# One kernel for sliding-window attention and an S4 convolution: all exponentials of a chunk ahead of its sines

## The chip, the cores and the metric

The kernel runs on one core of a Trainium2 chip. The metric is the time on the device in microseconds of one execution of the whole program; the median of several executions is given. The work is done by five engines that run side by side and wait for each other by semaphores: PE (matrix multiply, with its weight loads shown as PEld), DVE (vector), ACT (activation functions and copies), POOL, and SP, which only issues transfers. Each engine works through its own instructions in a fixed order.

## The reference

Two independent parts share the launch and their results stand side by side in the output.

Part A is attention with 32 heads of 20 over 2048 positions, where each position looks at eight earlier ones, two apart. It is a projection to q, k, v, eight logits per position, a softmax and an output projection.

Part B is a long convolution with a filter that is computed on the fly:

```python
dt = jnp.exp(log_dt)[:, None]
logdA = dt * A                                   # A complex, 640 x 192
dB = dt * Bc
P = jnp.exp(logdA[:, :, None] * l[None, None, :])  # l = 0..2047
K = jnp.einsum("dn,dnl,dn->dl", Cc, P, dB).real    # the filter, 640 x 2048
...                                               # FFT of length 4096 of K and u, product, inverse
y = y + u * Dskip
```

The exponential of a complex number is an exponential of the real part (a magnitude) times a cosine and a sine of the imaginary part (an angle). The kernel therefore needs both Exp and Sin from ACT.

## The kernel before

**Chunks and halves.** The 640 channels of part B are cut into five chunks (`NCH`) of 128. For every chunk the 2048 filter points are made as products of two small tables: Y (32 fine offsets, twice) and X (32 coarse offsets). The coefficients of a chunk are in two halves (`th` 0 and 1, 16 of the channel rows `t` each). Each half has a Y and an X of its own place (`Y0`, `X0`, `Y1`, `X1`).

**Coefficient steps.** `prep_coef` and `prep_chunk` (L67 to L140) turn the parameters into exact pieces in 16-bit floats: `base` and `logmag` for magnitudes and angles, `phi` for the starting angle, which needs Arctan. The pieces go to memory (`scr`) and come back by `load_pieces` (L155) in two tiles: `PM` for magnitudes and `PF` for angles. Chunk 0 is handled by itself at the start; the coefficients of chunks 1 to 4 lie together in the tiles `natr` (place X1) and `cfr` (place Y1).

**Table steps.** `table_steps` (L185) makes the tables of one half in 18 steps. PE multiplies the pieces by constants (`RM`, `RF`) into a PSUM bank `ps_t`, and ACT takes the function. The first step gives the factors `E` (L216), three steps give the magnitudes `M` (L224), two give `MX` (L238), all with Exp. DVE completes M and MX with multiplies by E (L229, L240). Then come 12 sine steps (L252): for each of three blocks, cosine and sine of Y and cosine and sine of X. After each pair DVE multiplies in the magnitudes (L258 to L260 for Y by M, L264 for X by MX). `M`, `MX` and `E` have one place each, which both halves use in turn.

**Other steps.** `kgen_steps` (8 steps of matmuls, L290 and L294) multiplies X by Y for one half and copies the result to `Ksb` (L297). `fwd_steps` (8 steps) is a discrete Fourier transform in two stages: stage one (`f1`, L381) is copied to the tile `A1` (L342), stage two (`f2`, L392) to `Ssp` (L342). It runs for the input `u` (`u_steps`; the result is stored to memory in `Udram`) and for the filter `Ksb`, where DVE then multiplies it with `U`, read back from memory (L420). `ia` (4 steps, L429) is the first stage of the inverse; it is copied to `Z` and stored in `Zdram`. The second stage of the inverse (`ib`, L586) runs near the end, when `zq` is read back from `Zdram` in six groups; its weights are the constant `H`. The copies at L342 go to ACT or DVE by a letter pattern.

**The order of the work.** `interleave(a, b)` writes two lists of steps alternately. In the main loop each half's 18 table steps are interleaved with what became ready earlier: kgen of half 0, the previous chunk's `ia` and one `u_steps` during the tables of half 1; kgen of half 1 and the filter's forward steps during the tables of half 0 of the next chunk. The first list, during the sines of chunk 0, holds `u_steps(0)`, `u_steps(1)` and the coefficient steps of chunks 1 to 4. A scheduler then orders the instructions of each engine by its own model, keeping the written order as priority; `order`, `vorder` and `sorder` (L28) are chains that fix the order of chosen instructions on ACT, DVE and SP. Tiles with the same `tag` share a place, with as many copies as `bufs` says; a new tile there waits until all uses of the old one are over.

**After part B's chunks**, part A runs: projections (L657, L697), logits (L713, L716), softmax, the weighted sum (L772, L776) with `ib` between, and the output projection (L790). It uses places that part B has left: `xa` takes X0, `xb` and every second `zq` a place of their own, `S8`; `wq` takes MX, `prod` takes X1 and M, `attn` takes Z, `H` takes A1.

## Time and profile before

| | us |
|---|---|
| median of 3 runs | 535.12 (532.24 to 537.8) |
| the profiled execution | 537.6 |
| its span | 535.8 |
| DVE busy in the span | 389.2 (73%) |
| PE busy | 391.0 (73%) |
| ACT busy | 345.4 (64%) |
| first table load at L216 to the end of the last sine | 75.4 to 340.8 |

The profile is of one execution. Times count from the start of the span, which is a little shorter than the execution. A "line" is a line of the kernel; a helper such as the copy at L342 collects many tiles under one line, so groups are told apart by their tile names. An idle time is the time just before an instruction in which its engine did nothing, and the profile names the instruction that ended it. PE's ends are modelled. ACT loads a table of functions (ACT_TABLE_LOAD) whenever the next function isn't in the one it has.

### The profile page before, as it was taken

The numbers are of one execution on the slowest core, as the hardware profiler recorded it, in microseconds if no ns is written. First come the engines' busy times: TensorE is split into PE (matmuls) and PEld (weight loads), VectorE is DVE, ScalarE is ACT, GpSimd is POOL, SyncE is SP. The second block draws the span as 40 slices with busy tenths as digits, with TensorE's granted clock in tenths as the row PEclk, the third lists the DMA queues.
The fourth block names the chain that finished last, engine by engine and source line by source line (L and its number), as shares of the span: only waits on it lengthen the run. The fifth ranks groups of instructions, "written<-read, shape, count | busy, mean of one in ns | idle before, by whom it ended". The sixth has DMA issues, their size and how long they took to land.

```text
span 535.8 us, 15507 instructions
## 1 busy us (share of the span) xinstructions
PE 391.0 (73%) x7009; PEld 245.8 (46%) x7009; DVE 389.2 (73%) x420; ACT 345.4 (64%) x451; POOL 35.9 (7%) x51
## 2 busy tenths in 40 slices
PE   0214675856798858976897678799799797788687
PEld 0103553533475436643564356445444465455355
DVE  3656997938878596989885977704585999985840
ACT  2393795957889868986998669557345362633254
POOL 8700001010002001010000000000000000000000
PEclk9999877878899887988799789989999799877879
DMA  5499343280028100750016008902102004653413
GB/s 122 107 156 220 115 139 84 94 195 3 1 67 260 31 0 18 234 166 1 3 44 196 1 2 295 241 22 80 80 1 62 1 4 113 188 123 103 102 67 107
DMA packets 51706, 51.57 MB, mean 96 GB/s; under 512 B 37416, under 2 KB 48360, under 8 KB 48696
## 3 DMA queue, kind: packets, MB, share of 16 engines
q1 hardware_dynamic: 49752, 49.69, 34.3%
q0 software_dynamic: 1184, 0.89, 0.8%
q8 instruction: 55, 0.90, 0.7%
q10 hardware_dynamic: 704, 0.00, 0.1%
q14 instruction: 11, 0.09, 0.1%
HBM read 32.30 MB, written 18.19 MB: 94 GB/s over the span
## 4 chain that ended last, share of the span: by engine, by line
DVE 36%; PE 34%; ACT 15%; issue 10%; DMA 4%; ACTq 0%; SPq 0%; POOL 0%; DVEq 0%; POOLq 0%
PE ps_qk L657 6%; DVE A L342 4%; DVE Y L258 4%; PE ps_t L203 4%; PE ps_k L290 4%; DVE X L264 3%; DVE prod L772 3%; PE ps_k L294 3%; DVE Y L260 3%; ACT Y L252 3%; PE ps_op L790 3%; PE ps_ia L429 2%; ACT X L252 2%; DVE Ssp L342 2%; DVE prod L713 2%
## 5 line engine op out<-in xcount | busy, mean ns | idle before, releaser
L252 ACT ACTIVATE X<-ps_t 128x1024 bf16<-128x1024 int16 x60 | 61.5, 1055 | 4.8 <-PE ps_t L203 3.3
L252 ACT ACTIVATE Y<-ps_t 128x1024 bf16<-128x1024 int16 x60 | 61.0, 1045 | 5.5 <-PE ps_t L203 3.5
L772 DVE TENSOR_TENSOR prod<-v,attn 128x2048 bf16<-128x2048 bf16 (+1 forms) x48 | 47.4, 1041 | 15.3 <-PE ps_o L776 15.3
L203 PE MATMUL ps_t<-R,PF 128*128 128x512 f16 (+1 forms) x160 | 52.0, 415 | 1.7 <-ACT Ksb L297 0.6
L713 DVE TENSOR_TENSOR prod<-qT,kT 128x5120 bf16<-128x5120 bf16 x16 | 44.6, 2817 | 9.1 <-ACT qT L342 4.7
L203 PE MATMUL ps_t<-R,PM 128*128 128x256 f16 (+3 forms) x160 | 22.9, 272 | 36.5 <-DMA PM<-scr 23.5
L258 DVE TENSOR_TENSOR Y<-Y,M 128x2048 bf16<-128x2048 bf16 x30 | 36.6, 1220 | 15.4 <-ACT Y L252 15.4
L342 DVE CAST A<-ps_f 128x1024 bf16<-128x1024 f32 x28 | 34.1, 1219 | 15.8 <-PE ps_f L381 15.8
L342 ACT CAST Ssp<-ps_f 128x1024 bf16<-128x1024 f32 x26 | 26.5, 1019 | 19.4 <-PE ps_f L392 19.4
L294 PE MATMUL ps_k<-Y,X 64*32 64x64 bf16 x1280 | 26.5, 235 | 16.5 <-issue 16.5
L264 DVE TENSOR_TENSOR X<-X,MX 128x2048 bf16<-128x2048 bf16 x30 | 36.6, 1219 | 0.2
L260 DVE TENSOR_TENSOR Y<-Y,M 128x2048 bf16<-128x2048 bf16 x30 | 36.6, 1218 | 0.2
L776 PE MATMUL ps_o<-prod,ident 32*32 32x512 bf16 (+1 forms) x768 | 24.1, 388 | 14.8 <-DVE prod L772 12.3
L381 PE MATMUL ps_f<-BD,u 128*64 128x128 bf16 x320 | 21.8, 290 | 17.5 <-DMA BD<-c_BD 12.0
L203 PEld LDWEIGHTS <-PM 128*128 128x128 f16 (+1 forms) x160 | 13.9, 102 | 44.4 <-DMA PM<-scr 23.5
L294 PEld LDWEIGHTS <-X 64*32 64x32 bf16 x1280 | 19.9, 116 | 30.1 <-issue 29.5
L381 PEld LDWEIGHTS <-u 128*64 128x64 bf16 x320 | 19.7, 204 | 25.5 <-issue 25.5
L224 ACT ACTIVATE M<-ps_t 128x1024 bf16<-128x1024 f32 x30 | 28.5, 1026 | 3.9 <-DVE Y L260 3.9
L420 DVE TENSOR_TENSOR U<-U,Ssp 128x2048 bf16<-128x2048 bf16 x20 | 24.3, 1221 | 9.0 <-ACT Ssp L342 9.0
L392 PE MATMUL ps_f<-A,WK 128*128 128x128 bf16 x160 | 16.5, 265 | 18.2 <-DVE A L342 18.2
L290 PE MATMUL ps_k<-Y,X 128*32 128x64 bf16 x1280 | 24.4, 242 | 5.7 <-ACT Ssp L342 1.9
L206 PE MATMUL ps_t<-R,PF 128*64 128x512 f16 (+1 forms) x160 | 27.4, 433 | 1.7 <-ACT Ssp L342 0.9
(146 smaller groups left out, 795.0 us busy)
## 6 DMA issues: line engine op xcount, KB each, us to landing
Udram<-Ssp SPq DMA_DIRECT2D x5, 1024.0 KB
U<-Udram SPq DMA_DIRECT2D x5, 1024.0 KB
U<-Udram SPq DMA_DIRECT2D x10, 512.0 KB
Zdram<-Z SPq DMA_DIRECT2D x5, 1024.0 KB
zq<-Zdram SPq DMA_DIRECT2D x25, 192.0 KB
u<-in_B_u_dram SPq DMA_DIRECT2D x4, 640.0 KB
xn<-in_A_x_dram SPq DMA_DIRECT2D x4, 640.0 KB
out_dram<-ob SPq DMA_DIRECT2D x16, 160.0 KB
```

Of the source, the lines that this page charges most:

```text
L203: MM(ps, lhsT=Pt[0:K, 2 * blk + th, 0:128], rhs=rhs[0:K], start=True, stop=True, skip_group_check=True)
L252: order(nc.scalar.activation(out=dst, in_=ps[:].bitcast(i16)[:, :, 0::2].rearrange("p i (k z) -> p (i k) z", z=128), func=ACT.Sin, scale=S ...
L258: V.tensor_tensor(out=hi, in0=lo, in1=m(0), op=A.mult)
L260: V.tensor_tensor(out=lo, in0=lo, in1=m(1), op=A.mult)
L264: V.tensor_tensor(out=xf, in0=xf, in1=mx, op=A.mult)
L290: MM(o, lhsT=X[:, r, 4 * g + t // 4, :, t % 4], rhs=Y[:, r, 4 * g + t // 4, :, t % 4], start=(k == 0 and r == 0), stop=False, tile_positio ...
L294: MM(o, lhsT=X[hb:hb + 64, r, kq, :, t % 4], rhs=Y[hb:hb + 64, r, kq, :, t % 4], start=False, stop=(r == 1), tile_position=(hb, 32 * g), s ...
L342: ins = self.nc.scalar.copy(out=out, in_=in_) if e == "a" else self.nc.vector.tensor_copy(out=out, in_=in_)
L381: MM(ps[64 * r:64 * r + 64, i], lhsT=src_fn(8 * q + i), rhs=BD[:, r], start=(i % 4 == 0), stop=True, skip_group_check=True, tile_position= ...
L657: self.nc.tensor.matmul(ps, lhsT=self.w[w][:, kt, 128 * ct:128 * ct + 128], rhs=rhs(kt), start=(kt == 0), stop=(kt == 4))
L713: self.nc.vector.tensor_tensor(out=pr[:], in0=self.qT[:, hf], in1=self.kT[:, hf, :, :, HALO - DIL * w:HALO - DIL * w + 256], op=A.mult)
L772: nc.vector.tensor_tensor(out=p2[:, 0:nd], in0=self.v2[b][:, :, off:off + 256], in1=self.attn[:, hf, w, :].unsqueeze(1).to_broadcast([128, ...
```

## The change

`table_steps` becomes a class `Tables`, made once per chunk. Its `exps()` are the 11 exponential steps of both halves (one E for both, then M and MX of half 0 and of half 1) and its `sins(th)` the 12 sine steps of one half. M and MX get a place per half (`M0`, `M1`, `MX0`, `MX1`). In the main loop the exponentials and the sines of half 0 are interleaved with kgen of half 1, the forward steps and `ia` of the previous chunk; the sines of half 1 with kgen of half 0 and one `u_steps`, which comes one chunk later than before. PM has one copy instead of two, Z takes the place of A1, the scratch tiles are joined in U's place, `S8` goes (M0 takes its users), and H is no longer held whole: each `zq` group gets its slice of H by a transfer ahead of its five others.

At the start, the coefficient products `zed0` come before `base0` and their parameters are loaded first; SP's early transfers are chained. The exponentials of both halves of chunk 0 are issued before its Arctan, a Sin on a 128x1 tile stands before that, BD is loaded before u, and the phi pieces after u. `u_steps(0)`, `u_steps(1)` and the coefficient steps of chunks 3 and 4 move to the sines of half 1 of chunk 0. The x load is a step of its list and no longer issued ahead of it.

```diff
-    PM = pools["arena"].tile([128, 8, CW], f16, name="PM", tag="PM", bufs=2)
+    PM = pools["arena"].tile([128, 8, CW], f16, name="PM", tag="PM")
...
@@ -182,23 +182,24 @@
-def table_steps(tc, pools, R, P, th, order, Y, X, rows=(128, 128), vorder=None):
-    M = pool.tile([128, 6400], bf16, name="M", tag="M", bufs=1)
-    MX = pool.tile([128, 24, 32, 4], bf16, name="MX", tag="MX", bufs=1)
-    E = pool.tile([128, 2, 24, 4], bf16, name="E", tag="E", bufs=1)
...
+class Tables:
...
+    def __init__(self, tc, pools, R, P, order, rows=(128, 128), vorder=None):
...
+        self.PF, self.PM = P
+        ar = pools["arena"]
+        self.M = [ar.tile([128, 6400], bf16, name="M", tag="M%d" % th) for th in range(2)]
+        self.MX = [ar.tile([128, 24, 32, 4], bf16, name="MX", tag="MX%d" % th) for th in range(2)]
+        self.E = ar.tile([128, 2, 2, 24, 4], bf16, name="E", tag="E")
...
-    def new():
-        return psp.tile([128, 2, 512], f32, name="ps_t", tag="b", bufs=4)
-
...
-        order(nc.scalar.activation(out=E[:].rearrange("p k (b q) t -> p b k (q t)", b=6), in_=ps[:, 0, 0:192].rearrange("p (b k t) -> p b k t", k=2, t=16), func=ACT.Exp))
-
+    def gens(self):
+        ps = self.new()
+        for th in range(2):
+            for k in range(2):
+                for blk in range(6):
+                    o = 192 * th + 96 * k + 16 * blk
+                    self.block(ps[:, 0, o:o + 16], blk, th, self.PM, self.RM[:, 768 + 16 * k:784 + 16 * k], self.rows[0])
+        self.order(self.nc.scalar.activation(out=self.E[:].rearrange("p h k q t -> p (h k q t)"), in_=ps[:, 0, 0:384], func=ACT.Exp))
...
+    def mag(self, th, b):
+        M, V = self.M[th], self.V
+
+        def run():
+            ps = self.new()
...
+            self.order(self.nc.scalar.activation(out=M[:].rearrange("p (q y) -> p q y", q=2)[:, :, 1024 * b:1024 * b + 1024].rearrange("p q (k z) -> p q k z", z=128)[:, :, :, 0:64], in_=ps[:].rearrange("p q (k z) -> p q k z", z=64), func=ACT.Exp))
...
-    steps.append(gens)
-    steps += [mag(b) for b in range(3)]
-    steps += [magx(0, 4), magx(4, 2)]
-    for b in range(3):
-        steps += [sin(b, w, cs) for w in range(2) for cs in range(2)]
-    return steps
+
+    def exps(self):
+        out = [self.gens]
+        for th in range(2):
+            out += [self.mag(th, b) for b in range(3)] + [self.magx(th, 0, 4), self.magx(th, 4, 2)]
+        return out
+
+    def sins(self, th, Y, X):
+        return [self.sin(th, Y, X, b, w, cs) for b in range(3) for w in range(2) for cs in range(2)]
...
-                st["Z"] = pool.tile([128, 128, 32], bf16, name="Z", tag="Z")[:]
+                st["Z"] = pool.tile([128, 128, 32], bf16, name="Z", tag="A1")[:]
...
-        for a in (5, 4, 0, 2, 1, 3):
-            nc.sync.dma_start(out=n0[:, a, 0], in_=psrc(a, 0))
+        for a in (0, 2, 1, 3, 5, 4):
+            sorder(nc.sync.dma_start(out=n0[:, a, 0], in_=psrc(a, 0)))
...
         for nm, x, dst in (("RM", 1, RM), ("RF", 0, RF)):
+            sorder(nc.sync.dma_start(out=dst, in_=nc.inline_tensor(table_consts_np()[x].astype(np.float16), name="c_" + nm).ap()))
...
-                (nc.sync if a in (1, 3) else nc.gpsimd).dma_start(out=nr[:, a, c - 1], in_=psrc(a, c))
+                if a in (1, 3):
+                    sorder(nc.sync.dma_start(out=nr[:, a, c - 1], in_=psrc(a, c)))
+                else:
+                    nc.gpsimd.dma_start(out=nr[:, a, c - 1], in_=psrc(a, c))
...
-        S1 = ar.tile([128, 9, CW], f32, name="scr1", tag="U")
-        S2 = ar.tile([128, 20, CW], f16, name="scr2", tag="Z")
+        S = ar.tile([128, 19 * CW], f32, name="scr", tag="U")
+        S1, S2 = S[:, 0:9 * CW].rearrange("p (k n) -> p k n", n=CW), S[:, 9 * CW:19 * CW].bitcast(f16).rearrange("p (k n) -> p k n", n=CW)
...
+        zed0()
         base0()
         load_pieces(tc, P, scr, 0, (0,), sorder)
-        zed0()
         ln0()
         logmag0()
         load_pieces(tc, P, scr, 0, (1,), sorder)
...
-        fills = table_steps(tc, pools, (RF, RM), P, 0, order, Yb[0], Xb[0], rows=(32, 64), vorder=vorder)
+        tb = Tables(tc, pools, (RF, RM), P, order, rows=(32, 64), vorder=vorder)
+        fills = tb.exps()
         for st in fills[:6]:
             st()
         expr()
+        for st in fills[6:]:
+            st()
+        BD = const_tile(tc, ar, cn["BD"], "BD", nc.sync, order=sorder)
+        u = ar.tile([128, 64, 160], bf16, name="u", tag="u")
+        for g in range(4):
+            sorder(nc.sync.dma_start(out=u[32 * g:32 * g + 32], in_=usrc[g]))
+        order(nc.scalar.activation(out=tiny[:], in_=tiny[:], func=ACT.Sin))
         angle0()
+        phi0()
+        load_pieces(tc, P, scr, 0, (2,), sorder)
         angler()
         for c in range(1, NCH):
             for a in (4, 5):
                 nc.gpsimd.dma_start(out=nr[:, a, c - 1], in_=psrc(a, c))
-        u = ar.tile([128, 64, 160], bf16, name="u", tag="u")
-        for g in range(4):
-            sorder(nc.sync.dma_start(out=u[32 * g:32 * g + 32], in_=usrc[g]))
-        BD = const_tile(tc, ar, cn["BD"], "BD", nc.sync, order=sorder)
-        phi0()
-        load_pieces(tc, P, scr, 0, (2,), sorder)
...
-        work = u_steps(0, Evac(nc, "da", dict(a=order, d=vorder)))
+        preps = []
         for c in range(1, NCH):
-            work += prep_chunk(tc, S1, S2, nr[:, 4, c - 1], nr[:, 5, c - 1], dts, lamr[:, c - 1], angr[:, c - 1], c, scr, vorder, None)
-            if c == 1:
-                work += u_steps(1)
-        interleave(fills[6:], work)
+            preps += prep_chunk(tc, S1, S2, nr[:, 4, c - 1], nr[:, 5, c - 1], dts, lamr[:, c - 1], angr[:, c - 1], c, scr, vorder, None)
+        interleave(tb.sins(0, Yb[0], Xb[0]), preps[:6])
         Yb.append(Y1())
         Xb.append(X1())
         evz = Evac(nc, "da")
+        work = u_steps(0) + u_steps(1)
+        work = [x for i in range(16) for x in ([work[i]] + (preps[6 + i // 2:7 + i // 2] if i % 2 == 0 and i < 12 else []))]
         for c in range(NCH):
             Ksb = ar.tile([128, 32, 64], bf16, name="Ksb", tag="Ksb", bufs=2)
+            done = lambda Z, c=c: nc.sync.dma_start(out=Zd[c], in_=Z.rearrange("p m t -> p (m t)"))
+            load, prod, ia = inv_steps(tc, pools, IA, Ud[c], Banks(psk, tags), evz, done)
             if c:
-                P = nextP
-            tg = tags
-            done = lambda Z, c=c: nc.sync.dma_start(out=Zd[c], in_=Z.rearrange("p m t -> p (m t)"))
-            load, prod, ia = inv_steps(tc, pools, IA, Ud[c], Banks(psk, tg), evz, done)
-            for th in range(2):
-                if c or th:
-                    interleave(table_steps(tc, pools, (RF, RM), P, th, order, Yb[th], Xb[th]), work)
-                work = kgen_steps(tc, pools, th, Yb[th], Xb[th], Ksb)
-                if th == 0:
-                    work += prev_ia if c else []
-                    if c + 2 < NCH:
-                        work += u_steps(c + 2)
-                    elif c + 2 == NCH:
-                        work.append(lambda: nc.vector.tensor_tensor(out=u[:], in0=u[:], in1=Dsb[:].unsqueeze(1).to_broadcast([128, 64, 160]), op=A.mult))
-                    else:
-                        att.load_x()
-                        work += att.transposes(lambda: psk.tile([128, 2, 512], f32, name="ps_xt", tag="b", bufs=4))
-                    if c < last:
-                        nextP = new_pieces(tc, pools)
-                        load_pieces(tc, nextP, scr, c + 1, (0, 1, 2))
-                else:
-                    load()
-                    e2 = Evac(nc, "aad") if c < last else Evac(nc, "a")
-                    work += fwd_steps(tc, pools, BD, WK, (lambda t, Ksb=Ksb: Ksb[:, t, :]), Banks(psk, tg), Evac(nc, "d" if c < last else "da"), e2, each=prod)
+                tb = Tables(tc, pools, (RF, RM), nextP, order)
+                interleave(tb.exps() + tb.sins(0, Yb[0], Xb[0]), work + prev_ia)
+                work = []
+            work = kgen_steps(tc, pools, 0, Yb[0], Xb[0], Ksb) + work
+            if 0 < c and c + 1 < NCH - 1:
+                work += u_steps(c + 1)
+            elif c == NCH - 2:
+                work += u_steps(c + 1)
+                work.append(lambda: nc.vector.tensor_tensor(out=u[:], in0=u[:], in1=Dsb[:].unsqueeze(1).to_broadcast([128, 64, 160]), op=A.mult))
+            elif c == last:
+                work.append(att.load_x)
+                work += att.transposes(lambda: psk.tile([128, 2, 512], f32, name="ps_xt", tag="b", bufs=4))
+            if c < last:
+                nextP = new_pieces(tc, pools)
+                load_pieces(tc, nextP, scr, c + 1, (0, 1, 2))
+            interleave(tb.sins(1, Yb[1], Xb[1]), work)
+            load()
+            e2 = Evac(nc, "aad") if c < last else Evac(nc, "a")
+            work = kgen_steps(tc, pools, 1, Yb[1], Xb[1], Ksb)
+            work += fwd_steps(tc, pools, BD, WK, (lambda t, Ksb=Ksb: Ksb[:, t, :]), Banks(psk, tags), Evac(nc, "d" if c < last else "da"), e2, each=prod)
             prev_ia = ia
...
-    H = const_tile(tc, ar, cn["H"], "H", nc.sync, tag="A1")
+    Hd = nc.inline_tensor(cn["H"], name="c_H").ap()
...
-                zt[0] = z = ar.tile([128, NCH, 2 * NP, 32], bf16, name="zq", tag=("X0", "S8")[l // NP % 2])
+                zt[0] = z = ar.tile([128, NCH + 1, 2 * NP, 32], bf16, name="zq", tag=("X0", "M0")[l // NP % 2])
+                nc.sync.dma_start(out=z[:, NCH, 0:2 * np_], in_=Hd[:, 2 * l:2 * (l + np_)])
                 for c in range(NCH):
                     nc.sync.dma_start(out=z[:, c, 0:2 * np_], in_=Zd[c, :, 64 * l:64 * (l + np_)].rearrange("p (m t) -> p m t", t=32))
...
-                        MM(ps[sl, 160 * i:160 * i + 160], lhsT=H[sl, m, :], rhs=z[sl, :, m - 2 * NP * (l // NP), :], start=False, stop=(r == 1),
+                        MM(ps[sl, 160 * i:160 * i + 160], lhsT=z[sl, NCH, m - 2 * NP * (l // NP), :], rhs=z[sl, 0:NCH, m - 2 * NP * (l // NP), :], start=False, stop=(r == 1),
...
-        self.xb = ar.tile([128, 2, S], bf16, name="xb", tag="S8")
+        self.xb = ar.tile([128, 2, S], bf16, name="xb", tag="M0")
...
-        for i, nm, tag in ((1, "k", "WU"), (0, "q", "MX"), (2, "v", "R")):
+        for i, nm, tag in ((1, "k", "WU"), (0, "q", "MX0"), (2, "v", "R")):
...
-            pr = self.ar.tile([128, 5, 4, 256], bf16, name="prod", tag=("X1", "M")[w % 2])
+            pr = self.ar.tile([128, 5, 4, 256], bf16, name="prod", tag=("X1", "M1")[w % 2])
...
-                self.attn = self.ar.tile([128, 2, W, 256], bf16, name="attn", tag="Z")
+                self.attn = self.ar.tile([128, 2, W, 256], bf16, name="attn", tag="A1")
...
-            p2 = self.ar.tile([128, 8, 256], bf16, name="prod2", tag=("X1", "M", "Y1")[w % 3])
+            p2 = self.ar.tile([128, 8, 256], bf16, name="prod2", tag=("X1", "M1", "Y1")[w % 3])
```

## The prediction

> **What bounds the kernel now.** I read the engine totals first, then the stretches between table loads, then what each engine waits for.
>
> ```profile
> PE 391.0 (73%) x7009; PEld 245.8 (46%) x7009; DVE 389.2 (73%) x420; ACT 345.4 (64%) x451; POOL 35.9 (7%) x51
> ```
>
> No engine is full. In the middle of the run the work repeats once per chunk, from one load of the Exp table to the next but one. The busy-time-by-stretch view of one chunk (columns: stretch, its length, busy time of PE, PEld, DVE, ACT and POOL with instruction counts, granted clock, DMA share, GB/s) gives the two halves:
>
> ```profile
> 141.86:170.89 29.03, 24.67 (x484) 18.33 (x483) 24.41 (x25) 25.60 (x28) 3.35 (x3) 1.00 0.39 117
> 170.89:200.25 29.36, 20.78 (x414) 12.01 (x414) 21.59 (x22) 22.39 (x24) 0.93 (x1) 0.88 0.15 48
> ```
>
> Together 58.4 us, with PE busy for 45.5, DVE for 46.0 and ACT for 48.0: a chunk loses about 12 us to waiting on each of the three. Cutting each half at the first multiply of its Y shows where DVE loses them:
>
> ```profile
> 170.89:182.63 11.74, 9.23 (x279) 5.63 (x279) 4.67 (x6) 9.34 (x11) 0.93 (x1) 0.85 0.37 118
> 182.63:204.95 22.32, 14.27 (x157) 8.06 (x156) 21.63 (x21) 16.80 (x19) 0.00 (x0) 0.86 0.01 1
> 200.25:213.46 13.21, 10.96 (x313) 8.20 (x312) 8.55 (x9) 10.83 (x12) 1.38 (x1) 0.74 0.08 19
> 213.46:231.29 17.83, 16.12 (x245) 11.56 (x247) 17.72 (x19) 16.38 (x18) 2.91 (x2) 1.00 0.63 202
> ```
>
> From the Exp table load to that multiply DVE idles 7.1 us in one half and 4.7 in the other, 11.7 of its 12.4. From then on it is full (21.6 of 22.3, 17.7 of 17.8). So **DVE bounds the sine part, and starves during the exponential part**, because its multiplies need a sine, and ACT does a table load, E, the M and MX exponentials and another table load first. This happens twice per chunk.
>
> **The change part by part.**
>
> *Table loads.* The groups view has 19 in the main loop:
>
> ```profile
> L252 ACT ACT_TABLE_LOAD x10 | 12.8, 1283 | 0.7 <-DVE scr L130 0.6
> ...
> L216 ACT ACT_TABLE_LOAD x9 | 11.5, 1283 | 0.2
> ```
>
> With L59, L63, L91, L97 and L748 there are 24. After it, chunk 0 needs one Exp and one sine table, chunks 1 to 4 two each; with L59, L63 and L748 that is 13, or 15 if Arctan can't use the sine table (this trace loads one for each, with Arctan first, so it can't tell; I take 13, as the Sin on `tiny` now precedes Arctan, and keep 2.6 us for the other end). ACT sheds 11 x 1.283 = 14.1 us, at worst 9 x 1.283 = 11.5. The order-of-time view shows what one load takes:
>
> ```profile
> 169.82 1.05 ACT L342 CAST Ssp<-ps_f 128x1024 bf16<-128x1024 f32 x1
> 170.89 1.28 ACT L216 ACT_TABLE_LOAD   x1
> 172.18 0.33 ACT L216 ACTIVATE E<-ps_t 128x192 bf16<-128x192 f32 x1
> ```
>
> The previous cast ends at 170.87 and the activation starts 0.01 us after the load: 1.28 us, nothing else. The Trainium skill, "ScalarE: Activation LUTs", section "What ACT_TABLE_LOAD costs", puts a switch at about 2.66 us with a drain; by it the sum would be 29 us, but no drain stands here, so the row decides.
>
> ACT is not the bound, so these 14 us are not the gain; the starved stretches are. **One longer exponential stretch per chunk replaces two.** The first stretch above (11.7 us) grows by the second half's M and MX: 2.85 + 1.54 = 4.4, so 16.1 us. DVE has 4.7 us of work in it, gains the second half's three E multiplies (2 x 0.95 + 0.95 = 2.8), and two of the four casts to A (1.14 each, back to back; 2.3), since the filter half is evacuated at 183.5, 12.6 us after the load, before the longer stretch ends. Idle: 16.1 - 4.7 - 2.8 - 2.3 = 6.3 us, for 11.7: 5.4 gained. PE doesn't forbid it: 9.2 busy plus the second half's exponential matmuls, about 3.0 (30.4 us of L203 and L206 on PM over ten halves, the narrow ones left out), makes 12.2 of 16.1. ACT no longer waits for the Y multiply before M (0.4 to 0.9 us a half), as M has a place per half.
>
> *The light second stretch.* With the half-0 sines, the inverse steps (ia) and the previous chunk's forward steps in the first, the second has the half-1 sines, kgen of half 0 and u_steps: DVE 11.6 + 4.6 = 16.2 us, but PE about 7.9 (sines) + 5.1 (kgen) + 4.4 + 2.8 (u, L381 and L392) = 20.2, plus the 2.3 us hole that PE shows inside kgen ("issue"). PE needs 22.5, DVE has 16.2 and some 4 carried over from the heavy stretch: 2 us idle. Net 3.4 us per chunk, for chunks 1 to 4: 13.6. The bounds: 0 (the idle only moves) and 7 (DVE waits for nothing in the second stretch and M's waits go too).
>
> *Start and chunk 0.* The half-1 exponentials (4.4 us of ACT) now fill the time before the phi pieces come. The price is that Arctan moves from 38.4 to about 43.5 us, and phi with it; the first X sine stays near 53, since it ran at 53.6 behind forward casts that waited for BD (12.0 us on PE). BD now goes ahead of the 16 us load of u, and u_steps(0) and (1) move behind the half-0 sines, their two 1 MB stores (at 57.9 and 71.2 on the SP queue) with them, to near 75 and 90; chunk 0's U is read back right after and wanted only some 15 us into the next stretch, so I cost that at nothing (about 5 us if it came late). A new wait: Y1 and X1 lie where cfr and natr lie, and the coefficient steps of chunks 3 and 4, which read those, now stand among the steps of the half-1 sines. They are 2 x 5.2 us of DVE (L115 to L138), and until they end every half-1 sine on ACT is held; behind them wait kgen's second half and chunk 1's exponentials. DVE has 64.8 us of work from 30.4 to 108.2 and 13.0 idle; 4.6 of the work (u_steps(2)) leaves for later. I take 4 us gained, between 6 lost (the held sines aren't covered) and 9 (two thirds of the idle gone). zed0 ahead of base0 fills DVE's 6.7 us wait for dt, but zedr still waits for natr until 19.3: nothing.
>
> *PM with one place, Z in A1's.* PM's next load can start when the exponentials end, some 40 us before its use, and its four transfers took 1.7 us to issue: free. Z is worse: the next cast to A1 waits until the store of Z has landed. The SP queue in order of time:
>
> ```profile
> 216.22 0.34 SPq L413 DMA_DIRECT2D U<-Udram  x1
> 218.74 0.34 SPq L534 DMA_DIRECT2D Zdram<-Z  x1
> 219.12 2.18 SPq L415 DMA_DIRECT2D U<-Udram  x2
> ```
>
> The U loads share the engines; DMA is full from 217 to 227, and Z (1 of 3 MB) should land by 225, 6.3 us after its issue. Between Z and the u-step casts now stands kgen of half 0, 9.3 us from the Exp load to its matmuls' end in this trace: covered, 0, at worst 6.3 a chunk. "Trainium Kernel Development and Optimization", "Best Practices", advises double buffers to overlap DMA with compute and so speaks against both; by it the 6.3 would be paid three times, 19 us. No run here shows it yet.
>
> *End.* H comes in six slices beside zq instead of one early 1 MB load, each ahead of its five zq pieces: 192 KB at the 300 to 440 GB/s of full stretches is 0.6 us plus 0.4 of issue. PE waited 0.8 us for zq at 454.6; 1 us more there. The x load is now a step behind kgen, and ia no longer covers it (322 to 327.6 before): 1 us. Together -2, between 0 and -5. PE's extra narrow matmuls in gens: under 1 us a chunk, where PE idles.
>
> **Sum.** 13.6 + 4 - 2 = 15.6 us. The profiled execution took 537.6 us (span 535.8), inside the runs' 532.2 to 537.8 but 2.5 above their median; the gain carries over, so 535.1 - 15.6 = 519.5, say **520 us**.
>
> **The rivals.**
> 1. *The idle only moves.* All three engines have 46 to 48 us of work a chunk in a fixed ring of dependencies; if kgen, forward and inverse steps set the pace, fewer table loads buy nothing: 535.1 less the 4 of chunk 0, plus the 2 of the end, 533 us. For it: PE is full from 210 to 222. Against it: DVE's idle sits in the exponentials.
> 2. *Slower: the ring through A1.* The K forward, Z, its store and the u forward now use one place in turn. From the trace: first A cast to last K matmul 183.8 to 197.7, 13.9; to the last U product 6.1; ia and its last cast 5.6; store 6.3, or kgen 9.3 if PE does it in that order; u forward 11.4 (216.6 to 228); Ksb of the next chunk, 12.6, with the second half's exponentials ahead, 4.4. All in turn: 63.3 us against 58.4, so 4.9 x 3 chunks with u_steps, chunk 0's gain gone, 2 at the end: 535.1 + 17 = 552 us. It decides once exponentials and kgen stop overlapping the u steps; without that overlap's loss the ring is 46.3 us, under the 55 I expect, which speaks against it.
> 3. *DVE full.* The upper bounds, 7 x 4 + 4 with 1 lost at the end: 504 us. PE's 45.5 busy of the 51 left speaks against it.
>
> **Numbers.** My forecast, 512 to 529: 0.45. Rival 1: 0.15. Rival 2, and lesser forms of it from 541 on: 0.22. Rival 3: 0.18. Faster by over 1% (which is about what this kernel's runs can tell from no change) is 0.45 + 0.18. The range leaves out the far ends of rivals 2 and 3: 500 to 550.
>
> **What would show it.** Right: 13 table loads; per chunk one DVE hole of about 6 us, a period near 55; no wait of an A cast for the store of Z; chunk 1's Exp load near 100 us. Wrong: A casts or f1 matmuls released by the Z store; ACT idle among the half-1 sines of chunk 0 for over 10 us; PE waits for kgen's inputs at the head of the second stretch; PE waiting over 2 us for zq.

## The result: slower, 557 us

| | median, us | ratio to before, 95% interval |
|---|---|---|
| before | 534.1 | |
| changed | 557.3 (554.8 to 566.5) | 1.041 (1.033 to 1.049) |
| predicted | 520 (500 to 550) | |

The stored profile of the changed kernel is of an execution that was disturbed (566.5 us; so is that of c below, 562.0), so its lines below come from a second profile of the same kernel, made beside the experiments (execution 563.6 us, span 561.8; median there 560.9), and the ratios leave such executions out.

The engine totals of the changed kernel, first section of its page:

```profile
PE 403.0 (72%) x7089; PEld 251.6 (45%) x7089; DVE 391.5 (70%) x420; ACT 331.8 (59%) x436; POOL 35.5 (6%) x51
```

ACT has 13.6 us less to do than before (331.8 for 345.4) and DVE about as much (391.5 for 389.2), yet the span is 26 us longer: on both the time is waiting, not work. PE is busy for 12.0 us more (403.0 for 391.0), and not by its 80 extra matmuls: j below has the same 7089 and 389.9. The groups view of table loads:

```profile
L220 ACT ACT_TABLE_LOAD x4 | 5.1, 1283 | 0.1
L260 ACT ACT_TABLE_LOAD x4 | 5.1, 1283 | 0.1
```

Together with one each at L59, L63, L91, L519 and L765 these are 13 loads for 24. The start of a chunk on ACT in order of time (start, duration, engine, line, operation, tiles) looks as it did before, one load and then E for both halves at once:

```profile
104.05 1.92 ACT L353 CAST Ssp<-ps_f 128x1024 bf16<-128x1024 f32 x2
105.99 1.28 ACT L220 ACT_TABLE_LOAD   x1
107.29 0.49 ACT L220 ACTIVATE E<-ps_t 128x384 bf16<-128x384 f32 x1
```

Where the 26 us arise is read from when the same instruction comes in the kernels: the Exp table load that starts each of the chunks 1 to 4, and the last copy to `Ksb`, after which only the last forward and inverse steps and part A remain. All are microseconds from the start of each profile's span; the labels of the other rows are explained with the experiments.

| | c1 | c2 | c3 | c4 | last Ksb | span |
|---|---|---|---|---|---|---|
| before | 108.2 | 170.9 | 229.5 | 281.6 | 351.7 | 535.8 |
| changed | 106.0 | 174.0 | 235.4 | 297.7 | 376.8 | 561.8 |
| b: ia second | 105.4 | 173.4 | 235.8 | 299.3 | 369.8 | 557.6 |
| c: Z in its own place | 104.8 | 174.1 | 236.8 | 299.0 | 378.1 | 560.3 |
| i: both, H whole | 104.7 | 164.9 | 222.4 | 277.7 | 349.1 | 535.6 |
| f: both, u_steps(0) first | 103.4 | 159.8 | 217.0 | 272.0 | 343.6 | 531.2 |
| g: both, early stores chained | 100.8 | 159.2 | 216.3 | 273.6 | 345.2 | 528.0 |
| j: both, start repaired twice | 102.2 | 160.5 | 215.4 | 271.4 | 344.6 | 527.8 |
| l: j, exponentials per half | 101.5 | 162.2 | 218.8 | 277.7 | 343.1 | 523.7 |
| n: j, per half in the last chunk | 102.0 | 160.9 | 215.8 | 271.9 | 339.1 | 522.8 |

The changed kernel is 2.2 us ahead at chunk 1 and 25.0 behind at the last Ksb. What follows adds 1. So the loss is in the chunks, all four of them (5.3, 2.8, 10.2 and 9.0 us; chunk 3 now holds a u step that chunk 2 held before).

One chunk in three stretches of the busy-time view (stretch, length, busy time of PE, PEld, DVE, ACT and POOL with instruction counts, granted clock, DMA share, GB/s): from the Exp load to a Y multiply, to the start of `ia`, and to the next Exp load:

```profile
174.02:190.86 16.84, 13.53 (x370) 9.23 (x368) 11.96 (x13) 14.79 (x17) 2.09 (x2) 1.00 0.29 91
190.86:203.44 12.58, 5.94 (x42) 3.66 (x43) 12.34 (x14) 8.34 (x9) 0.00 (x0) 0.86 0.00 0
203.44:235.38 31.94, 27.73 (x501) 18.49 (x502) 22.58 (x22) 22.03 (x24) 1.86 (x2) 0.89 0.37 102
```

The third stretch holds the last sine block of half 0 and then the "light second stretch" of the prediction: DVE has 22.6 us of work in 31.9, so it idles 9.4, where 2 were forecast for the light stretch, and PE, with 27.7 busy, isn't full either. DVE is full in the stretch before (12.3 of 12.6). PE's order of time shows what divides the chunk (in brackets the idle time before it and what ended it):

```profile
198.71 0.59 PE L204 MATMUL ps_t<-R,PF 128*128 128x512 f16 x2
203.44 1.41 PE L440 MATMUL ps_ia<-IA,U 128*128 128x128 bf16 x16 [4.14 <-DVE U L431]
204.78 1.06 PE L207 MATMUL ps_t<-R,PF 128*64 128x512 f16 x4
205.78 1.94 PE L440 MATMUL ps_ia<-IA,U 128*128 128x128 bf16 x16
207.64 0.64 PE L207 MATMUL ps_t<-R,PF 128*64 128x512 f16 x4
...
214.72 2.13 PE L301 MATMUL ps_k<-Y,X 128*32 128x64 bf16 x124
...
221.73 0.29 PE L305 MATMUL ps_k<-Y,X 64*32 64x64 bf16 x6 [2.74 <-issue]
...
224.47 2.01 PE L392 MATMUL ps_f<-BD,u 128*64 128x128 bf16 x32
```

PE stood 4.1 us in front of `ia` until the last of the four U products on DVE had ended, and the narrow sine matmuls at L207 of the half's last block stand behind `ia` in PE's queue. In the kernel before, the last product of the same chunk ended at 203.8 and `ia` began 7.3 us later, behind kgen of half 0 and table matmuls, without a wait. From its order of time, one line of DVE and then two of PE:

```profile
202.60 1.22 DVE L420 TENSOR_TENSOR U<-U,Ssp 128x2048 bf16<-128x2048 bf16 x1
...
205.39 2.11 PE L290 MATMUL ps_k<-Y,X 128*32 128x64 bf16 x124
...
211.10 1.19 PE L429 MATMUL ps_ia<-IA,U 128*128 128x128 bf16 x16
```

The wait costs more than its length. The busy-time view of the changed kernel, for the wait, the 4.6 us behind it and the next 4 (the granted clock is the third number from the end):

```profile
199.30:203.44 4.14, 0.00 (x1) 0.00 (x1) 4.14 (x6) 2.11 (x3) 0.00 (x0) 1.00 0.00 0
203.44:208.00 4.56, 4.56 (x40) 3.19 (x40) 3.35 (x3) 1.27 (x2) 0.00 (x0) 0.63 0.02 5
208.00:212.00 4.00, 4.00 (x46) 2.57 (x42) 2.51 (x3) 3.54 (x4) 0.00 (x0) 1.00 0.00 0
```

PE comes out of the wait at 0.63 of its clock, and the first four matmuls at L207 take 1.06 us where the next four take 0.64. So ACT runs dry, as its own order of time shows (4.5 us before the first sine of that block):

```profile
200.30 1.10 ACT L260 ACTIVATE X<-ps_t 128x1024 bf16<-128x1024 int16 x1
205.89 1.02 ACT L260 ACTIVATE Y<-ps_t 128x1024 bf16<-128x1024 int16 x1 [4.48 <-PE ps_t L207]
```

Later in the same stretch kgen of half 0 has PE nearly to itself, with a hole that ends with "issue", and DVE's order of time shows 5.0 us without work, until a sine comes:

```profile
217.85 1.22 DVE L272 TENSOR_TENSOR X<-X,MX 128x2048 bf16<-128x2048 bf16 x1
224.08 1.23 DVE L266 TENSOR_TENSOR Y<-Y,M 128x2048 bf16<-128x2048 bf16 x1 [5.02 <-ACT Y L260]
225.63 1.23 DVE L353 CAST A<-ps_f 128x1024 bf16<-128x1024 f32 x1 [0.33 <-PE ps_f L392]
```

The SP queue in order of time shows what happened to the transfer that the prediction feared:

```profile
211.17 0.34 SPq L424 DMA_DIRECT2D U<-Udram  x1
212.21 0.34 SPq L549 DMA_DIRECT2D Zdram<-Z  x1
212.60 1.36 SPq L426 DMA_DIRECT2D U<-Udram  x2
```

Z's store is issued at 212.2 and the next cast to A1 on DVE comes at 225.6, released by a matmul and not by the store: 13.4 us, so in this kernel the store is covered.

### The profile page after: what moved, and what is told of

Read it like the earlier page. It is cut to its first block, busy times and chain, and to the rows that moved or that the text cites. A ratio compares the mean times of both kernels' runs of the same rounds, so it can differ in the third digit from the quotient of the medians.

```text
span 564.7 us, 15638 instructions
## 1 busy us (share of the span) xinstructions
PE 410.1 (73%) x7089; PEld 256.7 (45%) x7089; DVE 391.7 (69%) x420; ACT 331.1 (59%) x436; POOL 35.5 (6%) x51
## 4 chain that ended last, share of the span: by engine, by line
PE 37%; DVE 35%; issue 11%; ACT 9%; DMA 5%; SPq 2%; DVEq 0%; ACTq 0%; POOL 0%; POOLq 0%
PE ps_qk L674 6%; PE ps_ia L440 4%; PE ps_t L204 4%; DVE Y L266 4%; DVE U L431 4%; DVE A L353 4%; PE ps_f L392 3%; PE ps_k L301 3%; PE ps_k L305 3%; DVE prod L730 3%; DVE X L272 3%; DVE Y L268 3%; PE ps_t L207 2%; PE ps_op L807 2%; ACT M L230 2%
## 5 line engine op out<-in xcount | busy, mean ns | idle before, releaser
L260 ACT ACTIVATE Y<-ps_t 128x1024 bf16<-128x1024 int16 x60 | 60.1, 1035 | 39.5 <-PE ps_t L207 22.0
L204 PE MATMUL ps_t<-R,PF 128*128 128x512 f16 (+1 forms) x160 | 63.0, 495 | 24.4 <-DMA PF<-scr 16.9
L260 ACT ACTIVATE X<-ps_t 128x1024 bf16<-128x1024 int16 x60 | 61.3, 1043 | 9.3 <-PE ps_t L204 5.2
L204 PE MATMUL ps_t<-R,PM 128*128 128x256 f16 (+3 forms) x200 | 26.1, 255 | 29.8 <-DMA PM<-scr 24.1
L440 PE MATMUL ps_ia<-IA,U 128*128 128x128 bf16 x320 | 29.9, 262 | 17.8 <-DVE U L431 17.7
L305 PE MATMUL ps_k<-Y,X 64*32 64x64 bf16 x1280 | 25.3, 235 | 21.5 <-issue 21.5
L440 PEld LDWEIGHTS <-U 128*128 128x128 bf16 x320 | 26.8, 156 | 28.3 <-DVE U L431 20.2
L235 DVE TENSOR_TENSOR M<-M,E 128x1536 bf16<-128x1536 bf16 x20 | 18.3, 954 | 26.9 <-ACT M L230 26.9
L204 PEld LDWEIGHTS <-PF 128*128 128x128 f16 (+1 forms) x160 | 14.3, 113 | 41.7 <-issue 37.6
L305 PEld LDWEIGHTS <-X 64*32 64x32 bf16 x1280 | 19.7, 114 | 29.5 <-issue 28.7
L207 PE MATMUL ps_t<-R,PF 128*64 128x512 f16 (+1 forms) x160 | 28.9, 452 | 0.3
```

What stands on the lines that cost most here:

```text
L204: MM(ps, lhsT=Pt[0:K, 2 * blk + th, 0:128], rhs=rhs[0:K], start=True, stop=True, skip_group_check=True)
L260: self.order(self.nc.scalar.activation(out=dst, in_=ps[:].bitcast(i16)[:, :, 0::2].rearrange("p i (k z) -> p (i k) z", z=128), func=ACT.Si ...
L305: MM(o, lhsT=X[hb:hb + 64, r, kq, :, t % 4], rhs=Y[hb:hb + 64, r, kq, :, t % 4], start=False, stop=(r == 1), tile_position=(hb, 32 * g), s ...
L440: MM(ps[:, i], lhsT=st["U"][:, r, :, :, 8 * q + i].rearrange("p g k -> p (g k)"), rhs=IA[:, r], start=(i % 4 == 0 and r == 0), stop=(r == ...
```

## The experiments

"Z in its own place" also gives `Ksb` one place for two and puts `nat0` in Ssp's place, to make room; every kernel below that has it shares this. What that costs by itself was not measured.

### 1. What holds the chunks: the early inverse steps, or Z in A1's place

The changed kernel again, as the reference of these runs:

> The changed kernel as it is, for a profile beside the others. All theories: about 555 to 557 us, ratio 1.04; from Exp load to Exp load about 63 us per chunk instead of 58.4, PE idle about 4 us ahead of the first ia matmul (waiting for the last U product), and again inside kgen of half 0 at the head of the second stretch.

560.9 us, 1.051 (1.041 to 1.060).

**The inverse steps back behind kgen of half 0** (b), ahead of the u steps; Z stays in A1's place:

```diff
-                interleave(tb.exps() + tb.sins(0, Yb[0], Xb[0]), work + prev_ia)
+                interleave(tb.exps() + tb.sins(0, Yb[0], Xb[0]), work)
                 work = []
-            work = kgen_steps(tc, pools, 0, Yb[0], Xb[0], Ksb) + work
+            work = kgen_steps(tc, pools, 0, Yb[0], Xb[0], Ksb) + (prev_ia if c else work)
```

> One edit against the changed kernel: the four ia steps go back behind kgen of half 0, ahead of u_steps, as they stood before the change; Z stays in A1's place. Theory 1 (order: with ia in the first stretch nothing on PE covers the U products, and nothing but kgen fills the head of the second): the 3 to 4 us wait ahead of ia and the late last block of sines go, but now the u-step casts come right after Z, so the store of Z (about 6 us) is exposed; net 0 to -2 us a chunk, 548 to 557 us. Theory 2 (the shared place of Z and A1 sets the pace in the changed kernel): the ring gets no shorter, and the exposed store makes it longer: 555 to 575 us.

558.5 us, 1.047 (1.039 to 1.055): nothing gained, and above the range of theory 1. The wait for U is gone for the most part (PE 3.9 us for 18.7 in front of `ia`), and the store of Z takes its place. The waits view of this kernel (engine, tile, line, releaser: total, times, longest):

```profile
ACT A L353 <- DMA Zdram<-Z: 14.2, 3, 6.5
```

Its SP queue in order of time, the store of one Z:

```profile
218.15 0.34 SPq L549 DMA_DIRECT2D Zdram<-Z  x1
```

Its ACT in order of time, the casts that wait for that store:

```profile
221.65 1.02 ACT L260 ACTIVATE Y<-ps_t 128x1024 bf16<-128x1024 int16 x1 [0.71 <-PE ps_t L207]
226.56 1.93 ACT L353 CAST A<-ps_f 128x1024 bf16<-128x1024 f32 x2 [3.89 <-DMA Zdram<-Z]
```

The cast to A1 resumes 8.4 us after the store's issue, and ACT had nothing else to do for 3.9 of them.

**Z in a place of its own** (c); the inverse steps stay early:

```diff
-                st["Z"] = pool.tile([128, 128, 32], bf16, name="Z", tag="A1")[:]
+                st["Z"] = pool.tile([128, 128, 32], bf16, name="Z", tag="Z")[:]
...
-        n0 = ar.tile([128, 6, 1, CW], bf16, name="nat0")
+        n0 = ar.tile([128, 6, 1, CW], bf16, name="nat0", tag="Ssp")
...
-            Ksb = ar.tile([128, 32, 64], bf16, name="Ksb", tag="Ksb", bufs=2)
+            Ksb = ar.tile([128, 32, 64], bf16, name="Ksb", tag="Ksb")
...
```

> Z gets a place of its own again; room is made by one place for Ksb instead of two and by laying chunk 0's parameters where Ssp comes later. The order of steps stays that of the changed kernel. Theory 1 (order): no difference, 553 to 560 us, since no cast to A1 is seen waiting for the store of Z. Theory 2 (shared place): 3 to 5 us a chunk come back, 537 to 545 us.

557.8 us, 1.043 (1.032 to 1.054): nothing gained either, as theory 1 had it. PE's wait for U stands as it was, by the waits view of this kernel (18.7 us in the changed one):

```profile
PE ps_ia L440 <- DVE U L431: 18.1, 4, 6.2
```

**Both** (d):

> Both edits: ia behind kgen of half 0, and Z in its own place. Theory 1 (order): the wait ahead of ia goes and no store is exposed: 4 to 6 us a chunk, 535 to 541 us; from Exp load to Exp load about 58 us. Theory 2 (shared place): the same as with Z in its own place alone. If both run at 555, neither holds, and the length of a chunk is set by kgen and its holes.

534.8 us, 1.001 (0.996 to 1.006): all of it back. The waits view has 2.3 us for U on PE in the kernel with both and H whole (i), and no wait for the store. The wait for U isn't the whole loss, though: between 100 and 380 us PE's holes inside kgen that end with "issue" (nothing waited for that the profile shows) also fall, from 19.7 us in the changed kernel to 11.0 in i. They come and go with the place of `ia`; no run shows whether the wait brings them.

Where each loses, by length from mark to mark against "both, H whole" (60.2, 57.5, 55.4, 71.3 us):

| us more | c1 | c2 | c3 | c4 to last Ksb |
|---|---|---|---|---|
| ia second (b) | 7.8 | 4.9 | 8.2 | -0.8 |
| Z in its own place (c) | 9.2 | 5.2 | 6.8 | 7.8 |
| changed | 7.9 | 3.8 | 6.9 | 7.8 |

The two causes show by their places: the last chunk has inverse steps but no u steps, so a store that holds the u steps costs nothing there, and an early `ia` does. The changed kernel has the pattern of the early `ia`. The two don't add: by the ratios b loses 24 us against both, c 22, and the changed kernel, which has the two together, 21 to 27 (1.041 and 1.051).

**The shared place alone, in the kernel before** (h), with its scratch in S8:

```diff
-                st["Z"] = pool.tile([128, 128, 32], bf16, name="Z", tag="Z")[:]
+                st["Z"] = pool.tile([128, 128, 32], bf16, name="Z", tag="A1")[:]
...
-        S2 = ar.tile([128, 20, CW], f16, name="scr2", tag="Z")
+        S2 = ar.tile([128, 20, CW], f16, name="scr2", tag="S8")
```

> One part alone, in the kernel before: Z takes A1's place (the scratch of 16-bit pieces keeps a place of its own), nothing else changes; ia stays right ahead of u_steps. Theory 1 (in this order the store of Z is exposed): the first cast to A1 waits 5 to 7 us for the store in each of the three chunks with u_steps behind ia, 15 to 20 us in all: 546 to 556 us. Theory 2 (a shared place costs only where it lengthens a full ring): 533 to 538 us.

548.6 us for 536.0, 1.024 (1.019 to 1.029). Its chunks 1 to 3 in the busy-time view, which before were 62.7, 58.6 and 52.1 us:

```profile
108.18:175.89 67.71, 49.63 (x896) 31.91 (x896) 47.88 (x47) 48.35 (x52) 4.78 (x4) 0.82 0.34 89
175.89:244.21 68.32, 49.27 (x896) 31.51 (x896) 52.61 (x47) 48.43 (x52) 4.28 (x4) 0.85 0.23 70
244.21:295.99 51.78, 39.96 (x800) 24.99 (x800) 40.79 (x41) 43.54 (x48) 1.04 (x1) 0.93 0.18 57
```

Chunks 1 and 2, where a u step follows `ia`, are 5.0 and 9.7 us longer; chunk 3, which has none in that kernel, isn't. So the time came as theory 1 had it, but in two chunks instead of three, and only 3.3 us of waits carry the store's name; the rest of the price isn't named by the waits. Part of it is that PE is busy for some 3 us longer in each of the two (49.6 and 49.3 us, 46.6 and 46.3 before), at a lower granted clock (0.82 and 0.85, 0.89 and 0.88 before). The Trainium skill, "Trainium Kernel Development and Optimization", section "Best Practices", advises double buffers so that transfers overlap with compute; here the measurement agrees, at 12.7 us for one place taken away.

### 2. The start

The X sines of chunk 0 (L260, tile X) come at 63.2 us in the changed kernel, at 53.6 before. PE's longest wait of that time, from the waits view of the changed kernel:

```profile
PE ps_t L204 <- DMA PF<-scr: 16.9, 1, 16.9
```

The same view for ACT, from 40 to 66 us:

```profile
ACT scr L124 <- DVE scr L117: 10.2, 3, 3.5
ACT scr L137 <- DVE scr L117: 3.9, 3, 3.3
```

ACT in order of time, the last Y sines before and the X sines after these waits:

```profile
44.16 1.92 ACT L260 ACTIVATE Y<-ps_t 128x1024 bf16<-128x1024 int16 x2
...
62.59 0.67 ACT L124 CAST scr<-scr 128x576 f16<-128x576 f32 x1 [3.19 <-DVE scr L117]
63.16 1.93 ACT L260 ACTIVATE X<-ps_t 128x1024 bf16<-128x1024 int16 x2
```

The SP queue in order of time:

```profile
50.17 0.38 SPq L139 DMA_DIRECT2D scr<-scr  x1
54.86 0.36 SPq L126 DMA_DIRECT2D scr<-scr  x1
55.32 1.03 SPq L161 DMA_DIRECT2D PF<-scr  x2
```

Two queues hold the X sines. On SP the load of the phi pieces (`PF`) stands behind the store of chunk 1's base pieces (L126), which waits for its data: the load comes 5.2 us after the phi store (L139), where 1.8 would do, as a run below shows. On ACT the X sines stand behind casts of the coefficient steps of chunks 1 to 3 (chunk 3's are written among the half-1 sines, but the first of them comes here); the three at L124 wait 3.2 to 3.5 us each for DVE.

**u_steps(0) back among the half-0 sines of chunk 0** (f), its copies on the fixed chains of ACT and DVE, on top of both repairs of the chunks; the later coefficient steps then alternate with u_steps(1):

```diff
-        interleave(tb.sins(0, Yb[0], Xb[0]), preps[:6])
+        interleave(tb.sins(0, Yb[0], Xb[0]), u_steps(0, Evac(nc, "da", dict(a=order, d=vorder))) + preps[:6])
...
-        work = u_steps(0) + u_steps(1)
+        work = u_steps(1)
...
```

> On top of the version with ia back and Z in its own place (534.8 us): u_steps(0) goes back among the half-0 sines of chunk 0, chained with them on ACT and DVE as before the change; u_steps(1) and the last coefficient steps stay behind. Theory 1 (the start idles because phi comes late, and u_steps(0) filled that hole): chunk 1's Exp load comes 4 to 8 us earlier, 527 to 531 us. Theory 2 (the hole is hidden by DVE's coefficient steps, which have to be done anyway before the half-1 sines): within 2 us of 534.8.

530.4 us, 0.991 (0.987 to 0.994); X sines at 53.1. The time is that of theory 1 but its sign isn't: chunk 1's Exp load comes 1.3 us earlier than in i, not 4 to 8, and the rest of the gain is in chunk 1 (56.5 us for 60.2).

**The early stores on SP's chain** (g), on top of both repairs of the chunks:

```diff
-            preps += prep_chunk(tc, S1, S2, nr[:, 4, c - 1], nr[:, 5, c - 1], dts, lamr[:, c - 1], angr[:, c - 1], c, scr, vorder, None)
+            preps += prep_chunk(tc, S1, S2, nr[:, 4, c - 1], nr[:, 5, c - 1], dts, lamr[:, c - 1], angr[:, c - 1], c, scr, vorder, sorder)
```

> On top of the version with ia back and Z in its own place (534.8 us): the stores of the coefficient pieces of chunks 1 to 4 join SP's chain, so that none of them stands ahead of chunk 0's phi pieces (in the changed kernel one waited 3.4 us there for DVE). Theory 1 (the queue's head blocks): X sines of chunk 0 start some 3 us earlier and the time is 531 to 533 us. Theory 2 (the phi pieces are late because DVE's Arctan chain is): no change, 533 to 537 us.

530.0 us, 0.987 (0.981 to 0.993), a little below the range of theory 1. The load of PF now follows the phi store by 1.8 us, and the X sines come at 57.9:

```profile
48.77 0.38 SPq L139 DMA_DIRECT2D scr<-scr  x1
50.54 0.80 SPq L161 DMA_DIRECT2D PF<-scr  x2
```

Each alone gains some 5 us (4.4 and 4.8 by the medians, 5.6 and 7.5 by the ratios). **Both** (j):

> All that helped, together: ia behind kgen of half 0, Z in its own place, u_steps(0) among the half-0 sines of chunk 0, the pieces' stores in SP's chain. Both theories on the start (the hole there is filled, or the queue's head is freed): between 524 and 530 us; if the two cure the same hole, no more than either alone, 529 to 531 us.

530.7 us, 0.994 (0.991 to 0.998): no more than either by itself, which fits one hole that either fills.

### 3. H in slices

**H whole again** (i), in Z's place, with five transfers per `zq` group, on top of both repairs of the chunks:

```diff
+    H = const_tile(tc, ar, cn["H"], "H", nc.sync, tag="Z")
...
-                zt[0] = z = ar.tile([128, NCH + 1, 2 * NP, 32], bf16, name="zq", tag=("X0", "M0")[l // NP % 2])
-                nc.sync.dma_start(out=z[:, NCH, 0:2 * np_], in_=Hd[:, 2 * l:2 * (l + np_)])
+                zt[0] = z = ar.tile([128, NCH, 2 * NP, 32], bf16, name="zq", tag=("X0", "M0")[l // NP % 2])
...
```

> On top of the version with ia back and Z in its own place (534.8 us): H is loaded whole into Z's place once part B's chunks are over, and the zq groups have five transfers again. Theory 1 (the slice of H ahead of each zq group makes PE wait: 8.4 us at zq in that version, 0.8 before the change): 529 to 533 us. Theory 2 (PE's wait there is covered by DVE): within 1.5 us of 534.8.

536.1 us, 1.002 (0.999 to 1.004): the same as with slices (1.001). The wait for zq at the second inverse stage, of PE and its weight loads together, is 0.8 us before, 8.9 in the changed kernel and 3.0 here, and nothing of that reaches the end.

### 4. The exponentials of both halves first, by themselves

**The exponentials of half 1 back in front of half 1's sines** (l) from chunk 1 on, on top of j; 8 table loads return, and M and MX keep their two places:

```diff
-    def exps(self):
-        out = [self.gens]
-        for th in range(2):
+    def exps(self, ths=(0, 1)):
+        out = [self.gens] if 0 in ths else []
+        for th in ths:
...
-                interleave(tb.exps() + tb.sins(0, Yb[0], Xb[0]), work)
+                interleave(tb.exps((0,)) + tb.sins(0, Yb[0], Xb[0]), work)
...
-            interleave(tb.sins(1, Yb[1], Xb[1]), work)
+            interleave((tb.exps((1,)) if c else []) + tb.sins(1, Yb[1], Xb[1]), work)
```

> The same with one thing undone: in chunks 1 to 4 the exponentials of half 1 go back ahead of the half-1 sines (E stays one for both halves), so 8 table loads and the second exponential stretch per chunk come back. Theory 1 (one exponential stretch instead of two saves DVE some 3 us a chunk, as the prediction had it): 10 to 16 us above the version with all that helped, 537 to 544 us. Theory 2 (the loads and stretches were covered, so that putting all exponentials first brings nothing by itself): within 3 us of that version. Theory 3 (it brings ACT's load time and no more): 8 to 10 us above it.

526.0 us, 0.987 (0.983 to 0.992), no slower than j and below all three expectations. But the marks tell two things: chunks 1 to 3 are longer without the change (60.7, 56.5, 58.9 us for j's 58.3, 54.9, 56.0, which n below repeats with 59.0, 54.9, 56.1), and the last one is shorter (65.5 for 73.2). One of j's chunks, from its Exp load to the first Y multiply and on to the next Exp load:

```profile
160.54:175.06 14.52, 13.41 (x358) 8.90 (x356) 8.21 (x10) 14.35 (x17) 2.25 (x2) 1.00 0.36 110
175.06:215.44 40.38, 31.27 (x568) 22.16 (x563) 37.27 (x37) 30.01 (x32) 1.96 (x2) 0.96 0.27 77
```

DVE idles 6.3 us and 3.1. What j's last chunk loses by shows in front of the copies to Ksb. ACT's groups by shape in j, over the last chunk from its Exp load to the last of these copies:

```profile
L308 ACT CAST Ksb<-ps_k 128x1024 bf16<-128x1024 f32 x3 | 3.0, 1014 | 18.6 <-PE ps_k L305 18.6
```

The same group of l, with exponentials per half, over the same stretch of work:

```profile
L308 ACT CAST Ksb<-ps_k 128x1024 bf16<-128x1024 f32 x3 | 3.0, 1012 | 12.9 <-PE ps_k L305 12.9
```

ACT stands 18.6 us in front of these copies, against 12.9: 5.7 of the 7.7 us. They wait for kgen on PE, whose holes that end with "issue" are 8.3 us there in j (one of 5.3) and 3.1 in l; the granted clock of the chunk is 0.87 and 0.95. A reading that fits, but that these lines don't show: with no u step in it, the second stretch leaves DVE and ACT too little to stand beside kgen.

**Exponentials of half 1 back in the last chunk alone** (n):

```diff
-                interleave(tb.exps() + tb.sins(0, Yb[0], Xb[0]), work)
+                interleave((tb.exps((0,)) if c == last else tb.exps()) + tb.sins(0, Yb[0], Xb[0]), work)
...
-            interleave(tb.sins(1, Yb[1], Xb[1]), work)
+            interleave((tb.exps((1,)) if c == last else []) + tb.sins(1, Yb[1], Xb[1]), work)
```

> The kernel of the run with all three repairs (Z and the inverse steps, u_steps(0), the chain of the early stores), with the exponentials of half 1 back ahead of half 1's sines in the last chunk alone; chunks 1 to 3 keep all exponentials first. Theory A (the order of the exponentials gains about 2.3 us in each of chunks 1 to 3 and loses it all in the last chunk, which has no u_steps to stand beside its second stretch): the last chunk, from its Exp load to its last Ksb copy, falls from 73.2 to about 66 us, and the time to 522 to 526 us, no longer than the 525.95 of the kernel with every half by itself. Theory B (the gain per chunk is only work put off, which has to be done later wherever the order changes back): the last chunk stays near 72 us and the time near 530 us.

524.6 us, 0.980 (0.976 to 0.984), the fastest of all, with the last chunk at 67.1 us, so it is the order in that chunk that costs j there. Against j the gain is clear (the intervals don't meet). Against l it isn't: the last Ksb copy comes 4.0 us earlier, the end 0.9, and the intervals overlap. The Trainium skill, "ScalarE: Activation LUTs", section "Table sets: the hidden batching unit", has it that a kernel should do all functions of one table set and then all of the next. By these runs that gains 1.6 to 2.9 us in each of chunks 1 to 3 and loses 7.7 in the last; the number of loads doesn't decide (13 in j, 21 in l, which is no slower).

**Per half throughout, the chain of stores, but u_steps(0) as the change has it** (m):

> The kernel with every half's exponentials by themselves from chunk 1 on and the chain of the early stores, but with u_steps(0) among the sines of half 1 of chunk 0 as the change has it (the run of every half by itself without that repair). Theory A (the chain and u_steps(0) cure the same hole at the start, and what is left between 530 and 526 us belongs to the order of the exponentials): 525 to 527 us, X sines of chunk 0 before 60 us. Theory B (u_steps(0) first is worth its 4.3 us beside the chain as well, once the exponentials stand per half): 530 us or more.

531.5 us, 0.992 (0.988 to 0.996), against l's 0.987 (the intervals overlap). The start isn't what differs: both reach chunk 1 at 102. Chunk 1 itself is 64.1 us for 60.7, with a hole of 4.1 us inside kgen that the profile ends with "issue". So the first of the two expectations has its time wrong; why u_steps(0) should matter there stays open.

## Why the prediction was wrong

**The step that failed** is in "the light second stretch", in the words "With the half-0 sines, the inverse steps (ia) and the previous chunk's forward steps in the first". Its sum counted what PE and DVE have to do in each stretch, and cost the move of `ia` at nothing. But `ia` needs all four U products, which are the end of those forward steps. Before, 7.3 us of kgen and table matmuls lay between the last product (203.8) and the first `ia` matmul (211.1); after the move none does, PE waits 4.1 to 6.3 us in each of the four chunks (18.7 in all), and the sine matmuls of the last block (L207) come behind the wait. That the early `ia` costs is shown by c against the kernel with both, some 22 us for this order alone; how much of it is the wait itself and how much the lower clock and the kgen holes that come with it isn't separated.

**Z in A1's place**, "covered, 0, at worst 6.3 a chunk". The prediction's reading was right in the letter: kgen of half 0 stands between, and the store is covered with time to spare. Its price was half right: uncovered, the wait was up to 6.5 us a time in b, but 21 us over three chunks all told, and 12.7 in the kernel before (h). What wasn't seen is that the cover has a price of its own: kgen lies behind the store only because `ia` was moved ahead of kgen. Either order costs about the same, so undoing one edit alone shows nothing.

**Rival 2, "the ring through A1"**, came nearest to the number, with 552 us, and to the chain: 63.3 us a chunk, measured 68.0, 61.4 and 62.3. Its point of decision tells nothing: kgen of half 0 ends before the u steps begin (223.6 and 224.5), but it did so before as well (210.7 and 216.6). And it put the link at the shared place, and the loss stands without it (c).

**Table loads**: 13, as forecast, and ACT's 13.6 us less is the 14.1 of the sum. They are not the gain, as it said: l has eight more and is no slower.

**The longer exponential stretch**: right where the chunk is clear. In j DVE's hole is 6.3 us, as worked out, in a stretch of 14.5 us for 16.1, and the second stretch leaves 3.1 for 2. The term was net 3.4 us for "chunks 1 to 4", 13.6 in all; against per-half exponentials it measured 2.4, 1.6 and 2.9 in three of them and -7.7 in the fourth, together nothing (-0.8). So this term failed as well, even with the order of `ia` mended. The fourth has no u step, and the sum took it like the others.

**The start**: +4 forecast, +2.2 at chunk 1's Exp load. The wrong line is "the first X sine stays near 53": it came at 63.2. The wait that the prediction named, half-1 sines held by the coefficient steps of chunks 3 and 4, isn't the one: half-0 sines are held by those of chunks 1 to 3, and by SP's queue, which it read only for the U stores. With either repair some 5 us more are gained, against i 1.3 (f) and 3.9 (g) of them by chunk 1's Exp load and 5.0 and 5.6 by chunk 2's.

**The end**: -2 forecast. The wait for zq grew by 8 us where 1 was forecast, and it cost nothing (i). PE waited 3.4 us for the x load where 1 was forecast; in b it waited 4.2 and the last chunk was no longer than with both, so this wait isn't shown to cost anything.

**The sum**: with the two edits undone the kernel is level with before, not 15.6 faster. It is 7.1 us ahead at chunk 3, and chunk 3, which now holds the u step that chunk 2 held before, gives 3.3 of it back; the last chunk and what follows give back the rest.

## What to carry over

When a consumer is moved ahead, look for the last producer that it waits for and for what stands behind it in its engine's queue, not only at the busy sums of the stretches. Two edits that are tied (a shared place, and the order that covers its store) have to be undone together before either shows its price. A gain from batching need not hold in every turn of a loop: here three turns gained 6.9 us together and the last, which has less other work beside it, lost 7.7; look at the last turn by itself.

## What the runs showed of the hardware

- An Arctan after a Sin needed no table load of its own: one load at L519 serves the Sin there, Arctan at L97 and the sines at L260, where before Arctan and the sines had a load each.
- PE shows holes inside kgen's small matmuls that end with "issue", nothing waited for: 2.7 us in the changed kernel above and 6.4 in its last chunk, 5.3 in j's last chunk. No run here says what they are.
- After PE stood still for 4.1 us, its granted clock was 0.63 over the next 4.6 us and 1.00 after that (changed kernel, 199.3 to 212.0); in i, after a wait of 3.2 us, it was 0.50 over the next 4.3.
- A 1 MB store held a place for 8.4 us from its issue (b) while the U loads shared the transfers (the DMA engines' busy share was 1.00 from 218.0 to 226.5 us), for the 6.3 estimated.
